# Layer 2's second product in seven products of sums, for two of its three superblocks

## The chip, the cores and the metric

The kernel runs on one core of a Trainium2 chip. Its engines work side by side, each through its own instructions in order: PE (TensorE) multiplies matrices, with its weight loads shown as a row of their own (PEld); DVE (VectorE), ACT (ScalarE) and POOL (GpSimd) work on elements; SP (SyncE) issues nearly all DMAs. The metric is the device time of one execution in microseconds (us). The kernel before takes 886.72 us, the median of 3 runs (886.31 to 887.06).

## The reference

Windowed attention over q, k, v (4 batches, 8 heads, 576 positions, 64 per head) gives x of 2304 tokens by 512. Two layers follow, each with weights 512x2048 and 2048x512:

```python
h = x @ w_in;  r = np.maximum(h, 0);  x = (r * r) @ w_out            # layer 1
h = x @ w_in2; g = h * np.tanh(log1p(exp(h)));  out = g @ w_out2     # layer 2
```

Everything is float32. A product of two float32 numbers is made of three matmuls: each operand is split into a high part (rounded to float32r) and a low part (the rest), and high x high, high x low and low x high are added.

## The kernel before, in words

The first 500 us are attention and layer 1, with the weights of layer 2 being unpacked and split beside them and stored to DRAM (`w1d`, `w2d`; `c_split`, `c_store`). Layer 2 is the loop at L1250. Its 2304 tokens are three superblocks of 768 (s = 0, 1, 2; "superblock one" is s = 0), and each superblock takes eight turns (g = 8s + m). Turn g makes one eighth of the hidden layer, two tiles of 128 features, for all 768 tokens.

- First product (`product`, L1121): it is already done as seven products of sums for eight, on 2x2 blocks: two tiles of features by two halves of 384 tokens (TH). Each product is 6 matmuls of 384 columns into one PSUM bank, and DVE and ACT combine the seven to four blocks. The sums of the weights come ready from `w1d` (`ring1_load`, four DMAs a turn: `ra`, `rb`, `rc`, `rd`, 1.84 MB together, for the turn after next); the sums of x are made ahead of a superblock by `x_prepare`, in 20 small jobs (`run_jobs`) of loads, POOL subtractions (L1055), ACT roundings (L1060) and DVE low parts (L1064).
- PSUM banks of the products: `p`, `h`, `o4`, `o5` in turn for g = 0, then `p` and `h` alone. The other six banks (`o0` to `o5`) hold the accumulators of the second product.
- Activation (`mish`, `mish_low`): ACT writes Mish twice, once rounded, once whole, and DVE subtracts (L1158) to get the low part.
- Second product (`o_chunk`, L1162): turn g does the 12 chunks of turn g-1, each 3 matmuls of 512 columns (L1172, L1173, L1174); stationary is a 128x128 piece of the activation, moving are the weights `vh`, `vl` (`ring2_load`). The list `share` spreads them between the seven products. So PE alternates between products of 6 matmuls and chunks of 3. Turn 24 has the last 12 chunks alone.
- Output: at the end of a superblock's last chunks (turn 8 and 16) `o_evac` copies six accumulators in pairs (ACT the even ones, DVE the odd ones) and stores them; `o_last` does it for the last superblock.

The order on every engine and on SP's queue is the order in which the program writes the instructions; waits are set by the data.

Of the kernel before, what the change touches and what calls it, by code (L numbers as in the profile page):

```python
# [8 lines left out]
F32 = mybir.dt.float32  # L9
# [9 lines left out]
P = 128  # L19
# [14 lines left out]
def two_layers(  # L34
# [37 lines left out]
    x1d = dp.tile([KC, P, NT], F32, name="x1d")  # L72
    w1d = dp.tile([FC // 2, P, 7 * 2 * 256], F32, name="w1d")
    w2d = dp.tile([FC, P, 2 * DM], F32, name="w2d")
    wsd = dp.tile([FC // 2, 2, P, 2 * DM], F32, name="wsd")

    def w_tile(dtype, hl, fc, name):
# [735 lines left out]
    def c_sums(i):  # L813
# [8 lines left out]
        tt(s3, a[:, 0:256], b[:, 0:256], op=ALU.subtract)  # L822
        tt(s4, a[:, 256:512], s2, op=ALU.subtract)

    def c_split(key, dst, first=0):
        f = wf.pop(key)[:, first:]
        n = f.shape[-1]
        hi = ap["c"].tile([P, DM], F32R, tag="c", name=f"c{len(wf)}", bufs=4)[:, 0:n]
        nc.scalar.copy(hi, f)
        late.append((f, hi, dst))  # L830

    def c_store():
        while kept:
            f, hi, dst = kept.pop(0)
            n = f.shape[-1]
            nc.sync.dma_start(out=dst[:, 0:n], in_=hi.bitcast(F32))
            nc.sync.dma_start(out=dst[:, n : 2 * n], in_=f)

# [5 lines left out]
    def c_tick1():  # L844

        i = made["at"]
        if i == 0:
            c_load(0)
        k, part = i // 4 * 4, i % 4
        if part == 3:  # L850
            c_split(k + 1, w2d[k // 2])
            a = wf[k]
            c_split(k, w1d[k // 4, :, 0:1024])
            wf[k] = a
        elif part == 0 and k:
            c_split(k - 2, w1d[k // 4 - 1, :, 1024:1536], 256)
            c_split((k - 2, 0), w1d[k // 4 - 1, :, 1536:2560])
        elif part == 1 and k:
            c_split(k - 1, w2d[k // 2 - 1])
            c_split((k - 2, 1), w1d[k // 4 - 1, :, 2560:3584])  # L860
        if i < NW:
            c_lower(i)
# [150 lines left out]

    def x_tile(s, name, part):
        k = 2 * KINDS.index(name) + part
        if s == 1:
# [91 lines left out]
    def ring2_load(m, g):  # L1108
        for e in range(2):
            k, pair_ = 2 * (g % 2) + e, []  # L1110
            for z, hl in enumerate("hl"):
                t = xp.tile([P, 512], F32R, tag=f"x{hl}{k}", name=f"v{hl}{g}_{e}")
                nc.sync.dma_start(
                    out=t.bitcast(F32), in_=w2d[2 * m + e, :, z * DM : (z + 1) * DM]
                )
                pair_.append(t)
            ring2[g, e] = pair_

# [1 line left out]

    def product(g, s, k, a, x):  # L1121
        banks = ((ps_b, "p"), (ps_h, "h"), (ps_b, "o4"), (ps_b, "o5"))
        pool, tag = banks[turns["p"] % (4 if g == 0 else 2)]
        turns["p"] += 1
        ps = pool.tile([P, 512], F32, tag=tag, name=f"p{k}_{g}")[:, 0:TH]
        w, (hi, lo) = ring1[g][a], xcs[s, x]
        terms = [(z, t, c) for z, t in ((0, hi), (0, lo), (1, hi)) for c in range(2)]
        for n, (z, t, c) in enumerate(terms):
            nc.tensor.matmul(  # L1129
                ps, w[:, z, c * P : (c + 1) * P], t[c], start=n == 0, stop=n == 5  # L1130
            )
        return ps
# [62 lines left out]
    def o_last(k):  # L1195

        ev = stg.tile([P, DM, 2], I32, tag="wraw", name=f"ev1_last{k}", bufs=4)
        ev = ev.rearrange("p c t -> p (c t)").bitcast(F32)
        b, at = 1 + (6 + k) // 4, (6 + k) % 4
        dst = out[b * S + at * P : b * S + (at + 1) * P, :]  # L1200
        if k != 2:
            (nc.scalar.copy if k % 2 else nc.vector.tensor_copy)(ev[:, 0:DM], acc[2, k])
            nc.sync.dma_start(out=dst, in_=ev[:, 0:DM])
            return
        h = stg.tile([P, DM], I32, tag="wf", name="ev1_half", bufs=4).bitcast(F32)[:, 0:256]
        nc.vector.tensor_copy(ev[:, 0:256], acc[2, k][:, 0:256])
        nc.sync.dma_start(out=dst[:, 0:256], in_=ev[:, 0:256])
        nc.scalar.copy(h, acc[2, k][:, 256:512])
        nc.scalar.dma_start(out=dst[:, 256:512], in_=h)

    j = NB - 1
    for fc in range(FC):
# [34 lines left out]


    todo = []
    for g in range(25):  # L1250
        s, m = divmod(g, 8)
        units_ = []
        if g == 0:
            relu2_b(pend)
            units_ = [lambda: m_out(*prev, 0), lambda: m_out(*prev, 1)]
            share = [0, 1, 1, 0, 0, 0, 0]
        else:
# [7 lines left out]
        if g == 24:  # L1265
            for h, (a, b) in ((1, (1, 2)), (0, (0, 3))):
                for c in range(3):
                    o_chunk(2, 23, todo[a], a, h, c)
                    o_chunk(2, 23, todo[b], 1 - a, h, c)
                    o_last(3 * h + c)  # L1270
            break
# [8 lines left out]
        def made_of(u, name):  # L1280
            a = mish(u, name)
            todo.append(a[0])
            lows.append(a)

        sub, add = ALU.subtract, ALU.add
        tt = nc.vector.tensor_tensor
        for k, (a, x) in enumerate(
            (
                ("a11", "b11"),
                ("a12", "b21"),  # L1290
                ("s2", "t2"),
                ("s3", "t3"),
                ("s1", "t1"),
                ("s4", "b22"),
                ("a22", "t4"),
            )
        ):
            ps = product(g, s, k, a, x)
            if k == 0:
                p1 = u_tile(f"p1_{g}")  # L1300
                nc.scalar.copy(p1, ps)
            elif k == 1:
                u = u_tile(f"c11_{g}")
                tt(u, ps, p1, op=add)
                made_of(u, f"g11_{g}")
            elif k == 2:
                u2 = u_tile(f"u2_{g}")
                tt(u2, ps, p1, op=add)
                done()
            elif k == 3:  # L1310
                u3 = u_tile(f"u3_{g}")
                tt(u3, ps, u2, op=add)
            elif k == 4:
                u = u_tile(f"c22_{g}")
                tt(u, ps, u3, op=add)  # L1315
                u4 = u_tile(f"u4_{g}")
                tt(u4, ps, u2, op=add)
                made_of(u, f"g22_{g}")
            elif k == 5:
                u = u_tile(f"c12_{g}")  # L1320
                tt(u, ps, u4, op=add)
                done()
                made_of(u, f"g12_{g}")
            else:
                u = u_tile(f"c21_{g}")
                tt(u, u3, ps, op=sub)
                done()
                made_of(u, f"g21_{g}")
            for _ in range(share[k]):
                units_.pop(0)()  # L1330
            if g == 0 and k == 3:
                m_evac(0, NB - 1)
            if m == 0 and g and k == 6:
                for n in range(3):
                    o_evac(s - 1, n)
            if 4 <= m < 8 and s < 2 and k in (1, 3, 4, 5, 6):
                run_jobs(1)
        done()
        if g == 0:
            jobs += x_prepare(1)  # L1340
        if g == 8:
            jobs += x_prepare(2)
        if g + 2 < 24:
            ring1_load((g + 2) % 8, g + 2)
        if g + 1 < 24:
            ring2_load((g + 1) % 8, g + 1)


# [83 lines left out]
```

## Time and profile before

| what | value |
|---|---|
| median of 3 runs | 886.72 us |
| profiled execution | 886.73 us, span 885.0 us, granted clock 0.999 |
| PE busy | 875.6 us, 99% of the span |
| DVE, ACT, POOL busy | 62%, 53%, 26% |
| DMA | 188 MB, mean 212 GB/s |

The span runs from the first to the last instruction; the execution's own time is 1.73 us longer. Busy times are sums over an engine's instructions. A PE that is busy all the time isn't a PE at its peak: the ends of matmuls are modelled, and what a matmul really takes is seen from the distance of one start to the next.

### The profile page before, as it was taken

Reading aid. Unit: us, or ns where it says so; the run is one execution under the profiler, and the core shown is the slowest. Engines: PE = TensorE matmul, PEld = TensorE weight load, DVE = VectorE, ACT = ScalarE, POOL = GpSimd, SP = SyncE. Lnnn points to the kernel's source line nnn. Section 1 sums busy time; section 2 is a strip of 40 time slices with the busy share of each in tenths; the row PEclk is TensorE's granted clock in tenths of the full one; section 3 lists DMA queues with packets and bytes.
Section 4 is the critical chain, followed back from the end, with each engine's and each line's share of the span. In section 5 each row is a group of like instructions: output and inputs, shape, how many; then the busy total and the mean of one; then the engine's idle time right before and its main releaser. Section 6 shows DMA issues by size and latency. Waiting matters only on the chain.

```text
span 885.0 us, 13898 instructions
## 1 busy us (share of the span) xinstructions
PE 875.6 (99%) x4642; PEld 753.7 (85%) x4642; DVE 549.6 (62%) x1221; ACT 471.7 (53%) x1108; POOL 226.0 (26%) x275
## 2 busy tenths in 40 slices
PE   8999999999999999999999999999999999999998
PEld 5588889998888788888888888888888888889987
DVE  6899997655697979977768243444444445433333
ACT  7888788775666666656655532333323334332332
POOL 4311144655665656642004000101000110000000
PEclk9999999999999999999999999999999999999999
DMA  8366694743875759754878765465494755566341
GB/s 301 96 220 202 201 317 149 261 153 124 280 241 176 241 171 326 273 171 157 302 235 287 292 243 211 171 236 188 144 319 145 270 181 204 188 230 223 142 156 71
DMA packets 90455, 188.03 MB, mean 212 GB/s; under 512 B 12304, under 2 KB 30352, under 8 KB 90384
## 3 DMA queue, kind: packets, MB, share of 16 engines
q1 hardware_dynamic: 90240, 187.02, 62.2%
q8 instruction: 37, 0.61, 0.3%
q14 instruction: 34, 0.28, 0.1%
q10 hardware_dynamic: 144, 0.13, 0.0%
HBM read 146.21 MB, written 40.89 MB: 211 GB/s over the span
## 4 chain that ended last, share of the span: by engine, by line
PE 84%; DVE 12%; issue 2%; ACT 1%; POOL 0%; DMA 0%; SPq 0%; DVEq 0%; POOLq 0%; ACTq 0%
PE p L1129 20%; PE h L561 17%; PE acc L1174 8%; PE acc L1173 8%; PE acc L1172 7%; PE o L593 6%; PE o L589 6%; PE o L590 6%; PE o L499 3%; DVE wf L108 3%; DVE wl L128 2%; PE pt L423 1%; PE sc L328 1%; PE sc L327 1%; DVE wf L105 1%
## 5 line engine op out<-in xcount | busy, mean ns | idle before, releaser
L1152 ACT ACTIVATE g<-c 128x384 fp32r<-128x384 f32 x96 | 50.5, 526 | 222.2 <-DVE c L1315 124.4
L589 PE MATMUL o<-g,wh 128*128 128x512 f32 (+1 forms) x320 | 118.5, 377 | 0.0
L590 PE MATMUL o<-g,wl 128*128 128x512 f32 (+1 forms) x320 | 115.9, 369 | 0.0
L1174 PE MATMUL acc<-vh,g 128*128 128x512 f32 x288 | 114.3, 397 | 0.0
L1173 PE MATMUL acc<-vl,g 128*128 128x512 f32 x288 | 113.8, 395 | 0.0
L1172 PE MATMUL acc<-vh,g 128*128 128x512 f32 x288 | 112.1, 389 | 0.0
L1055 POOL TENSOR_TENSOR t<-xb,xb 128x384 f32<-128x384 f32 x12 | 13.5, 1137 | 291.6 <-DMA xb<-x1d 230.1
L628 ACT ACTIVATE r<-h 128x512 f32<-128x512 f32 (+1 forms) x80 | 44.1, 552 | 81.3 <-PE h L561 77.6
L647 DVE TENSOR_TENSOR g<-gg,g 128x512 fp32r<-128x512 f32 (+1 forms) x80 | 64.0, 799 | 30.1 <-ACT g L642 21.2
L561 PE MATMUL h<-xh,wh 128*128 128x512 f32 (+1 forms) x320 | 81.5, 376 | 0.0
L593 PE MATMUL o<-g,wh 128*128 128x512 f32 (+1 forms) x320 | 79.5, 370 | 0.1
L561 PE MATMUL h<-xl,wh 128*128 128x512 f32 (+1 forms) x320 | 79.0, 369 | 0.0
L561 PE MATMUL h<-xh,wl 128*128 128x512 f32 (+1 forms) x320 | 78.8, 368 | 0.0
L459 POOL TENSOR_SCALAR_AFFINE_SELECT pT<-p 128x128 f32<-128x128 f32 (+2 forms) x80 | 53.8, 694 | 79.2 <-ACT p L447 78.9
L589 PEld LDWEIGHTS o<-g,wh 128*128 128x128 f32 x320 | 60.5, 189 | 9.8 <-issue 0.5
L590 PEld LDWEIGHTS o<-g,wl 128*128 128x128 f32 x320 | 60.4, 189 | 9.3
L593 PEld LDWEIGHTS o<-g,wh 128*128 128x128 f32 x320 | 56.5, 189 | 11.5 <-DVE g L647 1.5
L381 ACT ACTIVATE p<-p,st 128x128 f32<-128x128 f32 (+1 forms) x144 | 59.1, 413 | 13.2 <-DVE st L366 12.8
L561 PEld LDWEIGHTS h<-xl,wh 128*128 128x128 f32 x320 | 56.9, 189 | 10.5
L561 PEld LDWEIGHTS h<-xh,wl 128*128 128x128 f32 x320 | 56.9, 189 | 10.1
L257 POOL TENSOR_TENSOR ulo<-uraw,uhi 128x256 fp32r<-128x256 f32 (+1 forms) x48 | 47.0, 979 | 69.7 <-ACT uhi L256 47.1
L1174 PEld LDWEIGHTS acc<-vh,g 128*128 128x128 f32 x288 | 53.9, 187 | 11.5
(119 smaller groups left out, 1811.0 us busy)
## 6 DMA issues: line engine op xcount, KB each, us to landing
wraw<-in_w SPq DMA_DIRECT2D x64, 512.0 KB, 4.5
ra<-w1d SPq DMA_DIRECT2D x24, 512.0 KB, 5.9
rc<-w1d SPq DMA_DIRECT2D x24, 512.0 KB, 4.2
rd<-w1d SPq DMA_DIRECT2D x24, 512.0 KB, 5.9
vh<-w2d SPq DMA_DIRECT2D x48, 256.0 KB, 6.2
vl<-w2d SPq DMA_DIRECT2D x48, 256.0 KB, 6.3
uraw<-in_qkT SPq DMA_DIRECT2D x24, 320.0 KB, 4.7
uraw<-in_qkT SPq DMA_DIRECT2D x24, 256.0 KB, 5.4
```

The lines of the kernel that those rows point to most:

```text
L381: nc.scalar.activation(probs(i, s), probs(i, s), AF.Exp, bias=u.st[:, s : s + 1], scale=-1.0, accum_out=u.st[:, sums + s : sums + 1 + s],)
L459: nc.gpsimd.affine_select(out=u.pT[:, 0:heads, k : 2 * n : 2, :][:, :, a:], in_=p[:, 0:heads, a:n], pattern=[[0, heads * (n - a)], [0, P / ...
L561: nc.tensor.matmul(ph[:, 0:n], w[:, c * P : (c + 1) * P], xs[j, c][k][:, 0:n], start=t == 0, stop=t == len(terms) - 1,)
L589: nc.tensor.matmul(o, wh[:, ws], g[:, 0, r], start=start, stop=False)
L590: nc.tensor.matmul(o, wl[:, ws], g[:, 0, r], start=False, stop=False)
L593: nc.tensor.matmul(o, wh[:, ws], g[:, 1, r], start=False, stop=stop)
L647: nc.vector.tensor_tensor(g[:, 1, 0:n], gg[:, 0:n], g[:, 0, 0:n].bitcast(F32), op=ALU.subtract)
L1129: nc.tensor.matmul(ps, w[:, z, c * P : (c + 1) * P], t[c], start=n == 0, stop=n == 5)
L1152: nc.scalar.activation(t[:, 0, :], u, AF.Mish)
L1172: nc.tensor.matmul(o, hi, wh, start=first, stop=False)
L1173: nc.tensor.matmul(o, hi, wl, start=False, stop=False)
L1174: nc.tensor.matmul(o, lo, wh, start=False, stop=last)
```

## The change: what it does

Superblock one stays as it was. For superblocks two and three (s = 1, 2) the chunks of the second product are taken out of the turns; the second product gets a phase of its own (`products2`) behind the superblock's eight turns, and is made of seven products of 384 tokens by 1024 features by 256 outputs.

- The sums of the second weights (`t1` to `t4`) are made in turns 1 to 8 from the weights that superblock one has loaded (`t_prepare`: POOL sums, two ACT copies, two DVE subtractions, four stores a turn) and stored to `t2d`. `w2d` is laid out by halves of 256 columns, so its stores and superblock one's loads go in pieces of half the size.
- In superblocks two and three, Mish is written once, whole, into 16 block tiles. The sums of activations are made by POOL: `sums3` (two operations an eighth) in the turns, `sums_2` and `sums_4` in the phase. `high2` (ACT) and `low2` (DVE) split what the matmuls read.
- The phase has 56 steps q (7 products by 8 eighths). A step is 9 matmuls of 256 columns (3 token chunks by 3 terms), one load of weights 8 steps ahead (`t_load`, 256 KB), one `high2` 6 steps ahead, one `low2` 4 steps ahead, and in the first 16 steps one POOL sum. `combine` adds the seven products up from PSUM.
- The products of turns 9 to 23 take four banks in turn instead of two. x of the third superblock is prepared in the phase of the second one.

```diff
+    def t_prepare(m, k):                      # turn g = 1..8, m = g - 1, k = 0..6
+        ...
+                nc.gpsimd.tensor_tensor(b, h, l, op=ALU.add)           # k = 0, two of 512
+        ...
+                nc.gpsimd.tensor_tensor(o, a, b, op=sub)               # k = 1, 2, two of 256 each
+        elif k in (3, 4):
+            ...
+            nc.scalar.copy(hi, t_parts["t", z])
+        elif k == 5:
+            for z in range(2):
+                t, hi = t_parts["t", z], t_parts["h", z].bitcast(F32)
+                nc.vector.tensor_tensor(t, t, hi, op=sub)
+        else:
+            ...
+                    nc.sync.dma_start(out=dst.rearrange("k p c -> p k c"), in_=halves(src))
+    def sums3(s, m):
+        ...
+        nc.gpsimd.tensor_tensor(t, a, b, op=ALU.subtract)
+        nc.gpsimd.tensor_tensor(b, b, c, op=ALU.add)
+    def sums_2(s, m):
+        t = s3s[s, m]
+        nc.gpsimd.tensor_tensor(t, block(s, A21, m), block(s, A11, m), op=ALU.subtract)
+    def sums_4(s, m):
+        t = block(s, A21, m)
+        nc.gpsimd.tensor_tensor(t, block(s, A12, m), s3s[s, m], op=ALU.subtract)
+    ORDER2 = (("s3", "t3"), ("s1", "t1"), ("s2", "t2"), ("s4", "b22"), ("a11", "b11"), ("a12", "b21"), ("a22", "t4"))
+    def low2(s, q):                           # five tiles in turn
+        ...
+        nc.vector.tensor_tensor(lo, left(s, q), hi.bitcast(F32), op=ALU.subtract)
+    def terms2(s, q, o, c):
+        m = q % 8
+        hi, lo = (t[:, c * P : (c + 1) * P] for t in his[s, q])
+        w = ts2[s, q]
+        for z, (a, b) in enumerate(((hi, w[:, 0:256]), (hi, w[:, 256:512]), (lo, w[:, 0:256]))):
+            nc.tensor.matmul(o[c], a, b, ...)
+    def products2(s):
+        sums3(s, 7)
+        for q in range(3, 6):
+            high2(s, q)
+        low2(s, 3)
+        if s == 1:
+            jobs.extend(x_prepare(2))
+        owed = None
+        for n in range(7):
+            last = s == 2 and n == 6
+            o = bank2(s, n, last)
+            for m in range(8):
+                q = 8 * n + m
+                if last:
+                    continue
+                for c in range(3):
+                    terms2(s, q, o, c)
+                ...
+                    t_load(s, q + 8)
+                if q < 8:
+                    sums_2(s, q)
+                elif q < 16:
+                    sums_4(s, q - 8)
+                if q + 6 < 56:
+                    high2(s, q + 6)
+                if q + 4 < 56:
+                    low2(s, q + 4)
+                if m == 1 and owed:
+                    combine(*owed)
+                    owed = None
+                if m == 6:
+                    flush()
+                if s == 1 and q >= 4 and q % 2 == 0:
+                    run_jobs(1)
+            if last:
+                combine(*owed)
+                flush()
+                tail2(s, o)
+                return
+            owed = s, n, o
+        combine(*owed)
+    def tail2(s, o):                          # the last product, token chunk by token chunk
+        ...
+        for c in range(3):
+            for m in range(8):
+                terms2(s, 48 + m, o, c)
+            at = slice(c * 256, (c + 1) * 256)
+            nc.vector.tensor_tensor(t[:, at], t[:, at], o[c], op=ALU.subtract)
+            put(s, 1, 0, t, (c,))
@@ product
-        pool, tag = banks[turns["p"] % (4 if g == 0 else 2)]
+        pool, tag = banks[turns["p"] % (2 if 0 < g < 9 else 4)]
@@ the loop over turns
-    for g in range(25):
+    for g in range(24):
...
         def made_of(u, name):
+            if s:
+                a, e = blocks2[s, BLK[name[1:3]], m // 2], m % 2
+                nc.scalar.activation(a[:, e, :], u, AF.Mish)
+                return
...
-            if m == 0 and g and k == 6:
+            if g == 8 and k == 6:
                 for n in range(3):
-                    o_evac(s - 1, n)
+                    o_evac(0, n)
...
+            if 0 < g < 9:
+                t_prepare(g - 1, k)
...
+            if s and m and k == 0:
+                sums3(s, m - 1)
+            if s and m in (3, 4, 5, 6) and k in (1, 4):
+                t_load(s, 2 * (m - 3) + (k == 4))
+            if s and m == 7 and k in (2, 4, 6):
+                high2(s, k // 2 - 1)
+                low2(s, k // 2 - 1)
...
+        if s and m == 7:
+            products2(s)
```

## Rows read from the trace of the kernel before

**Rows 1.** Busy times by stretch: length, PE, PEld, DVE, ACT, POOL, clock, DMA share, GB/s.
```profile
560.00:600.00 40.00, 40.00 (x201) 35.90 (x200) 17.66 (x34) 13.74 (x28) 4.00 (x4) 1.00 0.69 243
```
**Rows 2.** The chain that ended last, 820 to 885 us, by line.
```profile
by line: PE p L1129 38.2%; PE acc L1174 19.0%; PE acc L1173 18.9%; PE acc L1172 18.6%; DVE ev_last L1206 0.7%; ACT ev_half L1208 0.6%; issue 0.1%
```
**Rows 3.** Timeline (start us, us, engine, line): turn 9's start, turn 24, the end.
```profile
637.59 1.21 PE L1129 MATMUL p<-x_b,ra 128*128 128x384 f32 x6
...
873.83 0.39 PE L1172 MATMUL acc<-vh,g 128*128 128x512 f32 x1
...
881.08 0.39 PE L1174 MATMUL acc<-vh,g 128*128 128x512 f32 x1
...
882.37 0.37 ACTq L1209 DMA_DIRECT2D out_x<-ev_half  x1
```
**Rows 4.** Timeline of PE in turn 0: products that follow one another.
```profile
508.39 1.20 PE L1129 MATMUL p<-x_t,rc 128*128 128x384 f32 x6
509.43 1.20 PE L1129 MATMUL p<-x_b,rd 128*128 128x384 f32 x6
```
**Rows 5.** Timeline of PE in layer 1: matmuls of 256 columns, first and eighth.
```profile
154.19 0.28 PE L589 MATMUL o<-g,wh 128*128 128x256 f32 x1
...
155.03 0.28 PE L590 MATMUL o<-g,wl 128*128 128x256 f32 x1
```
**Rows 6.** Timeline of weight loads, same stretch.
```profile
154.07 0.19 PEld L589 LDWEIGHTS o<-g,wh 128*128 128x128 f32 x1
154.19 0.19 PEld L590 LDWEIGHTS o<-g,wl 128*128 128x128 f32 x1
```
**Rows 7.** Timeline at the end of turn 8: copies and stores of superblock one, then ring1.
```profile
637.79 1.29 DVE L1182 COPY ev<-acc 128x512 f32<-128x512 f32 x2 [0.37 <-PE acc L1174]
...
638.57 0.96 SPq L1193 DMA_DIRECT2D out_x<-ev  x2
...
642.12 2.44 SPq L1188 DMA_DIRECT2D out_x<-ev  x4
...
644.65 0.54 SPq L1094 DMA_DIRECT2D ra<-w1d  x1
```
**Rows 8.** The page, part 6: KB each, median us from issue to landing.
```profile
ra<-w1d SPq DMA_DIRECT2D x24, 512.0 KB, 5.9
```
**Rows 9.** Timeline of POOL and DVE, layer 1: both with work queued.
```profile
463.56 2.44 POOL L1055 TENSOR_TENSOR t<-xb,xb 128x384 f32<-128x384 f32 x2 [52.88 <-PE o L593]
463.74 1.39 DVE L805 SCALAR_TENSOR_TENSOR wf<-wraw,wf 128x512 int32<-128x512 int32 x1
465.16 1.39 DVE L808 SCALAR_TENSOR_TENSOR wf<-wraw,wf 128x512 int32<-128x512 int32 x1
465.97 1.46 POOL L1055 TENSOR_TENSOR t<-xb,t 128x384 f32<-128x384 f32 x1
466.59 1.13 DVE L820 TENSOR_TENSOR s<-wf 128x256 f32<-128x256 f32 x1
467.50 1.09 POOL L1055 TENSOR_TENSOR t<-t,xb 128x384 f32<-128x384 f32 x1
467.75 1.13 DVE L821 TENSOR_TENSOR s<-s,wf 128x256 f32<-128x256 f32 x1
```
**Rows 10.** The same engines, 12 us later.
```profile
476.04 2.00 POOL L1055 TENSOR_TENSOR t<-xb,xb 128x384 f32<-128x384 f32 x1 [7.45 <-DVE x_t L1064]
476.48 0.69 DVE L866 TENSOR_TENSOR wf<-wf,c 128x512 f32<-128x512 f32 x1
```
**Rows 11.** Timeline of POOL and DVE in turn 4 of layer 2.
```profile
569.01 2.00 POOL L1055 TENSOR_TENSOR t<-xb,xb 128x384 f32<-128x384 f32 x2 [85.62 <-DMA xb<-x1d]
569.46 0.56 DVE L1315 TENSOR_TENSOR c<-p,u 128x384 f32<-128x384 f32 x1 [1.88 <-PE p L1129]
...
572.07 1.02 POOL L1055 TENSOR_TENSOR t<-t,xb 128x384 f32<-128x384 f32 x1
572.37 1.13 DVE L1158 TENSOR_TENSOR g<-c,g 128x384 fp32r<-128x384 f32 x1
```

More of the change, by code (lines that the diff above doesn't have):

```diff
@@ L1193, in o_evac @@
         nc.sync.dma_start(out=dst, in_=ev)
[L1195 to L1209, printed above, removed]
+    t_parts = {}
@@ new lines, in sums_2, with left @@
+    def sums_2(s, m):
[5 more added lines that the diff above has]
+    ORDER2 = (("s3", "t3"), ("s1", "t1"), ("s2", "t2"), ("s4", "b22"), ("a11", "b11"), ("a12", "b21"), ("a22", "t4"))
+    def left(s, q):
+        n, m = divmod(q, 8)
+        b = {"s1": A21, "s4": A21, "a11": A11, "a12": A12, "a22": A22}.get(ORDER2[n][0])
+        return s3s[s, m] if b is None else block(s, b, m)
@@ new lines, in high2 @@
+    def high2(s, q):
+        name = f"hi{s}_{q}"
+        if q < 3:
+            tag = ("st1", "st2", "st3")[q]
+            hi = ap["x"].tile([P, TH], F32, tag=tag, name=name).bitcast(F32R)
+        else:
+            hi = u_tile(name).bitcast(F32R)
+        nc.scalar.copy(hi, left(s, q))
+        his[s, q] = [hi]
+    def low2(s, q):
+        k, name = q % 5, f"lo{s}_{q}"
+        if s == 2 and q > 52:
+            lo = ap["x"].tile([P, TH], F32, tag=f"st{q - 52}", name=name).bitcast(F32R)
+        elif k < 3:
+            lo = ap["x"].tile([P, TH], F32R, tag="lo", name=name, bufs=3)
+        else:
+            lo = gp.tile([P, 512], F32, tag=("r", "gg")[k - 3], name=name)
+            lo = lo.bitcast(F32R)[:, 0:TH]
+        (hi,) = his[s, q]
+        nc.vector.tensor_tensor(lo, left(s, q), hi.bitcast(F32), op=ALU.subtract)
+        his[s, q].append(lo)
@@ new lines, in t_load @@
+    def t_load(s, q):
+        n, m = divmod(q, 8)
+        b = ORDER2[n][1]
+        if s == 2 and q > 53:
+            t = rp.tile([P, 1024], F32R, tag="ra", name=f"tt{s}_{q}")[:, 0:512]
+        else:
+            tag = f"x{'hl'[q % 2]}{q // 2 % 4}"
+            t = xp.tile([P, 512], F32R, tag=tag, name=f"tt{s}_{q}")
+        if b[0] == "t":
+            src = t2d[int(b[1]) - 1, m]
+        else:
+            src = w2d[2 * m + int(b[1]) - 1].rearrange("p (d c) -> p d c", d=2)[:, int(b[2]) - 1]
+        nc.sync.dma_start(out=t.bitcast(F32), in_=src)
+        ts2[s, q] = t
@@ new lines, in terms2, with bank2 @@
+    def terms2(s, q, o, c):
[3 more added lines that the diff above has]
+        for z, (a, b) in enumerate(((hi, w[:, 0:256]), (hi, w[:, 256:512]), (lo, w[:, 0:256]))):
+            nc.tensor.matmul(
+                o[c],
+                a,
+                b,
+                start=m == 0 and z == 0 and c in o[3],
+                stop=m == 7 and z == 2 and c in o[4],
+            )
+    def bank2(s, n, last):
+        if last:
+            b = [ps_o.tile([P, 512], F32, tag=f"o{c}", name=f"m{s}_{n}_{c}") for c in range(2)]
+            b.append(ps_b.tile([P, 512], F32, tag="o4", name=f"m{s}_{n}_2"))
+            return [t[:, 0:256] for t in b] + [(0, 1, 2), (0, 1, 2)]
+        k = n % 2 * 2
+        a, b = (ps_o.tile([P, 512], F32, tag=f"o{k + z}", name=f"m{s}_{n}_{z}") for z in range(2))
+        return [a[:, 0:256], a[:, 256:512], b[:, 0:256], (0, 2), (1, 2), a, b]
@@ new lines, in rows, with put, flush, combine @@
+    def rows(s, h, c):
+        q = 6 * s + 3 * h + c
+        b, at = 1 + (q - 6) // 4, (q - 6) % 4
+        return slice(b * S + at * P, b * S + (at + 1) * P)
+    def put(s, h, d, t, parts=range(3)):
+        for c in parts:
+            dst = out[rows(s, h, c), d * 256 : (d + 1) * 256]
+            nc.sync.dma_start(out=dst, in_=t[:, c * 256 : (c + 1) * 256])
+    puts = []
+    def flush():
+        while puts:
+            put(*puts.pop(0))
+    def combine(s, n, o):
+        tt, add, sub = nc.vector.tensor_tensor, ALU.add, ALU.subtract
+        two_ = ((o[5], slice(0, 512)), (o[6][:, 0:256], slice(512, 768)))
+        def fresh(k):
+            t = stg.tile([P, DM, 2], I32, tag="wraw", name=f"c2_{s}_{k}", bufs=4)
+            sums2[k] = t.rearrange("p c t -> p (c t)").bitcast(F32)[:, 0:768]
+            return sums2[k]
+        def each(f):
+            for ps, at in two_:
+                f(ps, at)
+        if n == 0:
+            t = fresh("a")
+            each(lambda ps, at: nc.scalar.copy(t[:, at], ps))
+        elif n == 1:
+            a, b, c = sums2["a"], fresh("b"), fresh("c")
+            each(lambda ps, at: nc.scalar.copy(b[:, at], ps))
+            each(lambda ps, at: tt(c[:, at], ps, a[:, at], op=add))
+        elif n == 2:
+            for k in "cba":
+                t = sums2[k]
+                each(lambda ps, at: tt(t[:, at], ps, t[:, at], op=add))
+        elif n == 3:
+            t = sums2["b"]
+            each(lambda ps, at: tt(t[:, at], ps, t[:, at], op=add))
+        elif n == 4:
+            d = fresh("d")
+            each(lambda ps, at: nc.scalar.copy(d[:, at], ps))
+            for k, h in (("c", 1), ("b", 0), ("a", None)):
+                t = sums2[k]
+                each(lambda ps, at: tt(t[:, at], ps, t[:, at], op=add))
+                if h is not None:
+                    puts.append((s, h, 1, t))
+        elif n == 5:
+            t = sums2["d"]
+            each(lambda ps, at: tt(t[:, at], ps, t[:, at], op=add))
+            puts.append((s, 0, 0, t))
+        else:
+            t = sums2["a"]
+            each(lambda ps, at: tt(t[:, at], t[:, at], ps, op=sub))
+            puts.append((s, 1, 0, t))
@@ new lines, in products2 @@
+    def products2(s):
[12 more added lines that the diff above has]
+                if last:
+                    continue
+                for c in range(3):
+                    terms2(s, q, o, c)
+                if s == 2 and q == 40:
+                    t_load(s, 54)
+                    t_load(s, 55)
+                if q + 8 < (56 if s == 1 else 54):
+                    t_load(s, q + 8)
[14 more added lines that the diff above has]
+                    run_jobs(1)
+            if last:
+                combine(*owed)
[4 more added lines that the diff above has]
+        combine(*owed)
@@ L1211, in two_layers @@
+    def tail2(s, o):
+        t = sums2["a"]
+        for q in range(54, 56):
+            high2(s, q)
+        for q in range(52, 56):
+            low2(s, q)
+        for c in range(3):
[4 more added lines that the diff above has]
+            put(s, 1, 0, t, (c,))
     j = NB - 1
@@ L1264, in two_layers @@
             share = [2, 2, 1, 2, 2, 1, 2]
[L1265 to L1271, printed above, removed]
+        else:
+            share = [0] * 7
         if g == 0:
@@ L1283, in made_of @@
             lows.append(a)
+        if s and m % 2 == 0:
+            for b in range(4):
+                blocks2[s, b, m // 2] = block_tile(s, b, m // 2)
         sub, add = ALU.subtract, ALU.add
```

71 lines of the change are left out of this document (60 added, 11 removed).

## The prediction

> **What bounds the kernel now.** I read the busy times of stretches of layer 2 first, then the chain, and last the timelines. In a 40 us stretch of layer 2 PE is busy all of it at a granted clock of 1.00 (2.4 GHz), with DVE at 44%, ACT at 34%, POOL at 10% and DMA at 0.69 [rows 1]. The chain agrees: but for 1.4%, its last 65 us are the products and the chunks [rows 2]. So a change gains what it takes from PE's stream of matmuls, as long as PE then waits for nothing; that is what has to be checked, since PE waits for almost nothing today.
>
> What a matmul costs is read from start to start. Products that follow one another take 1.04 us for 6 matmuls of 384 columns, 173 ns each [rows 4]. Matmuls of 256 columns take (155.03 - 154.19) / 7 = 120 ns [rows 5]. Matmuls of 512 columns take (881.08 - 873.83) / 32 = 226.6 ns in turn 24 [rows 3].
>
> **The gross gain.** From the first product of turn 9 at 637.59 to the end of the last matmul (881.08 + 0.23) the old PE stream takes 243.7 us [rows 3]. In its place come 15 turns of 7 products, 105 x 1.04 = 109.2, and two phases of 7 x 8 x 9 = 504 matmuls of 256 columns, 1008 x 0.120 = 121.0 [rows 4, 5]: 230.2 in all, 13.5 less. By the same prices the old stream would be 109.2 + 576 x 0.2266 = 239.7; the other 4.0 is what the alternation of products and chunks costs, and I count it as gone. Bounds of the new matmul's price: 120 ns, or what a matmul pays in today's turns on top: 4.0 over the 1170 matmuls of 15 turns, 3.4 ns, which makes 3.5 of 1008. I take 120: same size and type in rows 5, beside busy engines.
>
> Here a rule speaks against the change. The weight load is 188 ns long in its row, yet loads start 120 ns apart, so they lie beside the matmuls [rows 6]. The Trainium skill ("TensorE: Matmul & The Clock Gate", "LDWEIGHTS (loading the stationary operand)" and "Measured speedup vs the span model") gives 107 ns for a load of 128 columns and lets it overlap a matmul in flight only for another row group; by it I estimate 107 + 107 ns per matmul, 95 us over 1008 more than by the rows. Rows 5 and 6 contradict it.
>
> **What PE will wait for.**
>
> *Turn 9, 2.2 us.* Nine turns have made 63 products, and 63 mod 4 = 3, so turn 9's first product goes to bank `o5`, still accumulator 5 of superblock one. `o_evac` has DVE copy accumulators 1, 3 and 5 in that order, and accumulator 1 ends with the last matmul before 637.59. DVE starts at 637.79 and takes 1.29 for two [rows 7], 0.65 each: `o5` is free at 639.73 instead of 637.59. Before, the banks were `p` and `h` and this was hidden.
>
> *Turn 10, 1.8 us.* SP issues six output stores, then ring1 for turn 10 at 644.65 [rows 7]. Afterwards the last four stores start some 2.3 us earlier (a third copy waited for a buffer that Mish no longer takes), and behind them stand the four stores of `t_prepare`, 4 x 0.6 (2.44 / 4). `ra` goes out at about 644.6 as before, but turn 10 now begins at 639.8 + 7.28 = 647.1. At a median landing of 5.9 [rows 8] it comes at 650.5, 3.4 late; with an empty queue, at half of that time, 0.4. I take 1.8. From then on a turn needs 1.84 MB in 7.28 us, 252 GB/s, with `t_load` 288 over a superblock; 243 GB/s take 0.69 of the DMA engines, so some 350 are there [rows 1]. Hidden.
>
> *The port, 15.6 us.* This decides. With both engines loaded, POOL's subtraction of 384 columns and DVE's operations with two inputs in SBUF run one at a time. DVE's 463.74 takes 1.39, and each of the next three ends only after a POOL operation has ended; POOL's last three start before a DVE operation has ended and finish 0.9 after it [rows 9]. Four pairs take 463.56 to 468.88, 5.32, so 1.33 to 1.35 a pair, for DVE operations of 384 columns on the mean: POOL 0.92, DVE 0.43. In layer 2 it is the same: L1158, two SBUF inputs, takes 1.13 and ends 0.41 after POOL's at 573.09; L1315, with one input in PSUM, takes 0.56 beside POOL [rows 11]. The Trainium skill ("SBUF — State Buffer", "SBUF: two separate sides") states this as an exclusive lock of a shared port pair; what it leaves open is who goes next when both wait.
>
> `low2` has two SBUF inputs; so have POOL's sums. `combine` and the products' sums read PSUM and go free. A step of the phase lasts 9 x 0.120 = 1.08 and needs one `low2`; but from `sums3(7)` on POOL has 18 sums queued (2 + 8 + 8), none of which waits for PE. While they last, one `low2` comes every 1.35, and PE falls back 0.27 a step. The lead of `low2` is small at the start, since `low2` of step 2 stands behind the eighth turn's last Mish and POOL's first sum (0.3 late). Third superblock: 18 steps x 0.27 + 0.3 = 5.2. Second superblock: `x_prepare` adds four POOL sums, so 22 cycles, 30 us; and from step 10 on DVE has its low parts in between, two SBUF inputs too, three of which each take a whole cycle: 19 x 0.27 + 3 x 1.35 + 0.3 = 9.5; its second four sums come around step 30 and cost about 0.9 of the lead. 10.4. Below: if DVE, having an operation ready, always goes before POOL, as once in 476.48 [rows 10], POOL's sums move into the gaps. The third superblock then loses 0.4; in the second the last sum, which step 31 needs, comes after 22 x 0.92 and some 41 low parts x 0.43, 37.9 against 31 x 1.08 = 33.5, and I allow as much again for ACT, whose splits stand in order behind those of x: 8.0. Above: with POOL at its free duration of 1.02 [rows 11] a cycle is 1.45 and both grow by 0.10 / 0.27, to 14.3 and 7.1. I take alternation, which rows 9 show four times.
>
> *The end, -0.2 us.* `tail2` needs four `low2` and a `combine` in its first 3 us: 0.3 late. After the last matmul's start the old kernel needs 885.0 - 881.08 = 3.9, with two copies in a row before the last store is issued at 882.37 [rows 3]; now one subtraction of 256 columns: 0.5 less.
>
> *Costed at nothing.* Turns 1 to 8 get 6 POOL, 2 ACT and 2 DVE operations and 4 stores each. Their turn is 15.7 us long with DVE and ACT more than half idle [rows 1], and x's sums run there today without a wait of PE [rows 1, 11]. Without that cover, DVE's two would cost at most 8 x 1.3 = 10. A second Mish and one DVE subtraction per block go, from engines with slack: nothing gained. The split layout of `w2d` doubles the number of pieces and not the bytes: 0 with DMA at 0.69.
>
> **The sum.** -13.5 + 2.2 + 1.8 + 15.6 - 0.2 = +5.9. Against the profiled execution (span 885.0, and 1.73 around it, 886.73; the median is 886.72) that is 892.6 us.
>
> **Rivals.**
> - *DVE goes first.* The port costs 8.4: 885.4. For it rows 10; against it rows 9, where POOL gets its turn each time. Decides if `low2` rows of the first 20 steps last 0.5 and POOL's 1.5.
> - *The port costs nothing (faster).* POOL's sums drift behind the splits, or the lead of 4 to 5 low parts carries PE over: port 0.3, sum -9.4, 877.3. For it: DVE is needed for only 0.43 of each 1.08. Against it: POOL's 0.92 and DVE's 0.43 make 1.35 in every step, whoever is first, until the sums are done. It decides if fewer than some 6 steps run at more than 1.1.
> - *Slower still.* The new matmuls pay the 3.4 ns for their three-term pattern, or the turns of 7.28 us wait for ring1 by 0.23 each: 3.5 on the forecast, 896.1. For it: the 4.0 of today's turns, and 288 of some 350 GB/s. Against it: rows 5, and the share in rows 1.
> - *Weight loads in series.* If each matmul waits for its own load, 0.19 and not 0.12 is the pitch: 1008 x 0.07 = 71 on the forecast, 963. It is the mechanism of the skill's rule on loads. Rows 6 speak against it.
>
> **How the numbers follow.** Chances: forecast 0.46, DVE first 0.18, port free 0.24, slower still 0.10, weight loads 0.02. 0.2% of the time, 1.8 us, is about what a measurement can tell from no change: faster is under 884.9, slower over 888.5. Faster: 0.24 from the free port, 0.09 from DVE first, 0.04 from an overestimated forecast, 0.37. Same: 0.07 of DVE first and 0.04 of the forecast, 0.11. Slower: the rest, 0.52. Signs differ between the cases, so the forecast's own range is 888 to 897 (port 12 to 19, turn 10 0.4 to 3.4, not both at one end). The range for 8 in 10 is 876.5 to 898: it leaves out the lower part of the free port, the weight loads and the ends.
>
> **What would show it.** In the new trace: `terms2` matmuls 120 ns apart; PE idle 2.2 us before turn 9's first product, released by a DVE copy; `low2` at some 1.3 us a row in the first 20 steps of each phase and 0.56 later, PE released by it in each of these steps; the second superblock's phase 70 us long, the third's 65, against 60.5 without a wait. The prediction is wrong if the phases take 61 us, if `low2` does not lengthen beside POOL's sums, or if the products of turns 9 to 23 wait for ring1 or a bank in turn after turn.

## The result, and the profile after

The changed kernel takes 897.59 us (median of 4 runs, 893.8 to 898.25), the kernel before 886.89 (886.31 to 888.19): a ratio of 1.011, 95% interval 1.008 to 1.014. It is slower, by 10.7 us. The forecast was 892.6, slower as the likeliest sign, with 888 to 897 as its own range and 876.5 to 898 as the range for 8 in 10: the time lies in the wider one, 0.4 below its end, and 0.6 above the narrower. The profiled execution, the longest of the four, took 898.25 us with a span of 895.9, 10.9 more than the span before; the trace is accounted against these 10.9.

PE's waits, summed over the whole span (what waits, for whom: us in all, times, longest):

```profile
PE p L1139 <- DMA ra<-w1d: 3.9, 1, 3.9
PE m L1326 <- DVE lo L1303: 3.7, 3, 1.2
...
PE p L1139 <- DVE ev L1192: 2.0, 1, 2.0
...
PE p L1139 <- DVE c L1578: 1.4, 3, 0.7
```

All four are new; the first three stand in the prediction's sum, the fourth (behind the ends of turns 4 to 7) was costed at nothing. The list by waits is too short, though: a matmul that comes late because its weight load waited for `low2` is booked on PEld, and a slow clock is no wait at all. So I measure the losses in the timeline, from start to start.

The gross gain is there as forecast. First the timeline (start, us) of two products of turn 10, then the busy times of a stretch of the second superblock's phase (columns as in [rows 1]):

```profile
659.99 1.20 PE L1139 MATMUL p<-x_t,rd 128*128 128x384 f32 x6
661.03 1.20 PE L1139 MATMUL p<-x_t,rc 128*128 128x384 f32 x6
```

```profile
740.00:769.00 29.00, 29.00 (x244) 29.00 (x243) 22.89 (x44) 14.04 (x30) 7.08 (x4) 1.00 0.82 263
```

Products follow one another in 1.04 us as in [rows 4], and 244 of the new matmuls take 29 us, 119 ns each, as in [rows 5]; the numbers of loads (PEld) and matmuls (PE) are the same but for one. No turn of the third superblock waits for ring1 or for a bank: its eight turns, from 769.25 to 827.50, take 58.25, 7.28 each.

Now the end of turn 8, turn 9 and turn 10, the lines that answer to [rows 3] and [rows 7]. PE first, then SP's queue:

```profile
640.46 0.40 PE L1184 MATMUL acc<-vh,g 128*128 128x512 f32 x1
642.84 2.38 PE L1139 MATMUL p<-x_b,ra 128*128 128x384 f32 x12 [1.98 <-DVE ev L1192]
...
649.22 1.21 PE L1139 MATMUL p<-x_t,rb 128*128 128x384 f32 x6
654.37 4.18 PE L1139 MATMUL p<-x_b,ra 128*128 128x384 f32 x12 [3.95 <-DMA ra<-w1d]
658.35 1.80 PE L1139 MATMUL p<-x_t,rc 128*128 128x384 f32 x6
659.99 1.20 PE L1139 MATMUL p<-x_t,rd 128*128 128x384 f32 x6
```

```profile
642.73 3.32 SPq L1198 DMA_DIRECT2D out_x<-ev  x4
646.10 0.58 SPq L1240 DMA_DIRECT2D t2d<-th  x1
...
648.03 0.46 SPq L1240 DMA_DIRECT2D t2d<-t  x1
648.58 0.66 SPq L1106 DMA_DIRECT2D ra<-w1d  x1
```

Turn 9 starts 2.15 us after the last chunk's matmul ends (640.46 + 0.23 to 642.84). Turn 10 should have started at 649.22 + 1.04 = 650.26 and starts at 654.37, 4.11 late, 5.79 after its `ra` was issued. Behind this wait 18 matmuls take 5.62 us (654.37 to 659.99) in place of 3 x 1.04 = 3.12, another 2.50. That is the clock, as the busy times of this stretch, and of the first 12 matmuls alone, show:

```profile
650.00:660.00 10.00, 6.05 (x22) 5.76 (x21) 1.17 (x3) 2.05 (x4) 1.99 (x2) 0.66 1.02 366
654.40:658.30 3.90, 3.90 (x12) 3.90 (x13) 0.00 (x0) 0.48 (x1) 0.00 (x0) 0.50 1.02 403
```

The third number from the end is the mean granted clock, where 1.00 is 2.4 GHz and 0.50 the lower level of 1.2 GHz: 0.66 over the 10 us, and 0.50 over the first 12 matmuls behind the wait. The number behind it is the busy share of the DMA engines, here as good as all of them.

In the phases the reader should look at DVE and POOL together, at the start of the second superblock's phase:

```profile
702.70 7.04 DVE L1303 TENSOR_TENSOR lo<-s,hi 128x384 fp32r<-128x384 f32 x6 [0.99 <-ACT hi L1290]
709.67 9.09 DVE L1303 TENSOR_TENSOR lo<-a,hi 128x384 fp32r<-128x384 f32 x7
718.68 1.37 DVE L1076 TENSOR_TENSOR x_b<-xb,x_b 128x384 fp32r<-128x384 f32 x1
```

```profile
704.14 9.04 POOL L1270 TENSOR_TENSOR s<-a,a 128x384 f32<-128x384 f32 x7
713.15 2.61 POOL L1067 TENSOR_TENSOR t<-xb,xb 128x384 f32<-128x384 f32 x2
```

Seven `low2` take 718.68 - 709.67 = 9.01 us, 1.29 each, and seven POOL sums 713.15 - 704.14 = 9.01, also 1.29 each: one of each in turn, as in [rows 9]. PE needs a `low2` every 1.08. The phase of the second superblock takes 68.70 us (700.55 to 769.25), that of the third 65.14 (827.50 to 892.52 and one matmul); 504 x 0.120 = 60.48 would be without loss, so 8.2 and 4.7 are lost.

The whole account of the span, in us: -13.5 gross; +2.4 in turns 1 to 8 (from layer 2's first product to the last chunk's matmul 501.40 to 637.36 before, 502.06 to 640.46 now: 135.96 and 138.40); +2.15 turn 9; +4.1 and +2.5 turn 10 and its clock; +8.2 and +4.7 in the phases; -0.5 at the end (3.4 from the last matmul's start in place of 3.9); +0.7 ahead of layer 2, which stays unexplained (its first product starts between 500.4 and 502.6 in all traces of this study); +0.1 in turn 9's first products. The sum is +10.9.

### The profile page after: what moved, and what is told of

Same layout as the page of the kernel before. It is cut to its first block, busy times and chain, and to the rows that moved or that the text cites. A ratio compares the mean times of both kernels' runs of the same rounds, so it can differ in the third digit from the quotient of the medians.

```text
span 895.9 us, 15580 instructions
## 1 busy us (share of the span) xinstructions
PE 875.0 (98%) x5074; PEld 770.3 (86%) x5074; DVE 649.5 (73%) x1320; ACT 500.8 (56%) x1177; POOL 359.4 (40%) x387
## 4 chain that ended last, share of the span: by engine, by line
PE 78%; DVE 12%; DMA 4%; issue 2%; ACT 2%; SPq 1%; POOL 0%; DVEq 0%; POOLq 0%; ACTq 0%
PE h L562 17%; PE p L1139 16%; PE m L1326 13%; PE o L594 6%; PE o L590 6%; PE o L591 6%; PE o L500 3%; PE acc L1184 2%; PE acc L1183 2%; PE acc L1182 2%; DMA vl<-w2d 1%; PE pt L424 1%; DVE wf L109 1%; PE sc L329 1%; PE sc L328 1%
## 5 line engine op out<-in xcount | busy, mean ns | idle before, releaser
L1326 PE MATMUL m<-tt,hi 128*128 128x256 f32 x672 | 122.7, 283 | 0.2
L1326 PEld LDWEIGHTS m<-tt,hi 128*128 128x128 f32 x672 | 104.4, 191 | 0.7 <-issue 0.5
L1326 PE MATMUL m<-tt,lo 128*128 128x256 f32 x336 | 98.9, 294 | 4.0 <-DVE lo L1303 3.7
L1528 ACT ACTIVATE a<-c 128x384 f32<-128x384 f32 x64 | 33.5, 526 | 80.3 <-DVE c L1567 42.7
L1326 PEld LDWEIGHTS m<-tt,lo 128*128 128x128 f32 x336 | 64.0, 191 | 10.1 <-DVE lo L1303 9.7
L590 PEld LDWEIGHTS o<-g,wh 128*128 128x128 f32 x320 | 60.5, 189 | 9.8 <-issue 0.5
L1265 POOL TENSOR_TENSOR s<-a,a 128x384 f32<-128x384 f32 x16 | 16.6, 1037 | 124.4 <-ACT a L1528 124.4
```

The source lines that it names most:

```text
L590: nc.tensor.matmul(o, wh[:, ws], g[:, 0, r], start=start, stop=False)
L1326: nc.tensor.matmul(o[c], a, b, start=m == 0 and z == 0 and c in o[3], stop=m == 7 and z == 2 and c in o[4],)
L1528: nc.scalar.activation(a[:, e, :], u, AF.Mish)
```

## The experiments

Each ratio is to the kernel before, with its 95% interval.

**No sums.** The calls of `sums_2` and `sums_4` left out.

```diff
-                if q < 8:
-                    sums_2(s, q)
-                elif q < 16:
-                    sums_4(s, q - 8)
```

> The changed kernel without POOL's 16 sums in each phase (`sums_2` and `sums_4` are left out, so products three and four multiply unsummed blocks). Theory (POOL's sums and DVE's `low2` exclude each other): both phases lose their waits; the second superblock's phase falls from 68.7 to about 62 (x's four POOL sums stay), the third's from 65.0 to about 61, and the time falls by some 10 us, to about 887. Rival (the splits come late for another reason: ACT's order, the five low tiles, DVE's own load): the phases stay at 68 and 65, since neither the splits nor their number change.

Measured 885.11 us, 0.9976 (0.9962 to 0.9989). The phases take 61.2 and 61.4 us. So the 16 sums of each phase cost 7.5 and 3.8 us, 11.3 of the 12.9 that the phases lost. The other 0.7 and 0.9 are there without them, with x's sums still in the second superblock's phase.

**The same sums for nobody.** POOL does as many subtractions of the same size, into a tile that nothing reads (`sums_4` is changed in the same way).

```diff
-        t = s3s[s, m]
-        nc.gpsimd.tensor_tensor(t, block(s, A21, m), block(s, A11, m), op=ALU.subtract)
+        t = spare(s)
+        nc.gpsimd.tensor_tensor(t, block(s, A12, m), block(s, A11, m), op=ALU.subtract)
```

> As the run without the sums, but POOL does 16 subtractions of the same size per phase from two block tiles into a tile that nothing reads (the products read unsummed blocks, as in that run). Theory of the exclusion: the phases are as long as with the real sums, 68 and 64 to 65, and `low2` takes 1.3 us a row beside them. Rival (PE waits because the sums' data come late): phases of 61 to 62, as nothing waits for these sums.

Measured 895.42 us, 1.0096 (1.0081 to 1.0111); phases of 69.2 and 64.9 us. The loss is back though nothing depends on the sums: it is that POOL works there, not that its results come late.

**Turn 9's bank.** One more product is counted ahead of turn 9, so that its first product goes to bank `p` (64 mod 4 = 0) and not to `o5`.

```diff
+        if g == 9:
+            turns["p"] += 1
```

> One product number is skipped at turn 9, so that its first product goes to bank `p` instead of `o5`. Theory: the 2.0 us wait of PE before turn 9's first product goes. Turn 10 begins 2.1 us earlier and waits for `ra` as much longer (6 instead of 3.95), with the clock as low behind it: same time as the changed kernel within 1 us. Rival (the two waits add up independently): 2 us faster.

Measured 896.80 us, 1.011 (1.0094 to 1.0127): 0.8 below the changed kernel's median, less than its four runs differ among themselves. Turn 9 starts right behind the chunks, and turn 10 waits the longer:

```profile
646.27 1.21 PE L1139 MATMUL p<-x_t,rb 128*128 128x384 f32 x6
654.21 4.03 PE L1139 MATMUL p<-x_b,ra 128*128 128x384 f32 x12 [6.74 <-DMA ra<-w1d]
```

Turn 10 starts at 654.21 against 654.37: the two waits stand one behind the other, and the transfer sets the end of both.

**Ring1 for turn 10 ahead of the stores.**

```diff
             if g == 8 and k == 6:
+                ring1_load(2, 10)
                 for n in range(3):
                     o_evac(0, n)
...
-        if g + 2 < 24:
+        if g + 2 < 24 and g != 8:
```

> Ring1 of turn 10 is issued before superblock one's output stores and before the four stores of weight sums, instead of behind them. Theory: `ra` lands before turn 10, the 3.95 us wait and the 2.5 us at half clock behind it go: 6.4 us faster, about 891. Rival (DMA bandwidth, not the order, makes `ra` late): the wait moves to another part of ring1 or to turn 11, less than 2 us gained.

Measured 890.48 us, 1.0047 (1.003 to 1.0064): 7.1 us gained. No wait for `ra` is left; the one for the bank stays, and in this trace the clock falls behind it:

```profile
644.75 3.47 PE L1139 MATMUL p<-x_b,ra 128*128 128x384 f32 x12 [1.98 <-DVE ev L1192]
648.02 1.71 PE L1139 MATMUL p<-x_t,rc 128*128 128x384 f32 x6
649.56 1.20 PE L1139 MATMUL p<-x_t,rd 128*128 128x384 f32 x6
```

18 matmuls in 4.81 us in place of 3.12. This profiled execution took 894.41 us, the longest of six and 3.9 above their median, so the loss of clock need not be in the others. In the changed kernel's own trace the same wait of 1.98 cost next to nothing of clock (642.84 to 645.06 is 2.22 for 12, in place of 2.08).

**Both.**

> Both edits around turn 9 at once: the products of turn 9 begin in banks o4 and o5, and turn 10's ring1 load goes out ahead of the three stores. The one with the early load gained 7.1 us and still held the 1.98 us wait for the bank, with about 1.7 us of half clock behind it. If that rest comes from the bank wait, this gives 890.5 - 3.7 = 886 to 888 us with full clock from turn 9 on. Rival: as with the bank edit alone, another wait takes the place of the bank's, and the time stays at 890 to 891.

Measured 888.27 us, 1.0016 (1.0007 to 1.0026). Turn 9 begins with bank `p`, as in the run on the bank alone. A wait of 0.9 for turn 11's `ra` is all that is left around there, and the clock stays at 1.00. With turn 10's transfer out of the way the bank edit is worth 2.2 us, about the wait itself, where alone it brought nothing that stands clear of the scatter. Turns 9 and 10 together cost 9.3 us.

**The sums on DVE.**

```diff
-        nc.gpsimd.tensor_tensor(t, block(s, A21, m), block(s, A11, m), op=ALU.subtract)
+        nc.vector.tensor_tensor(t, block(s, A21, m), block(s, A11, m), op=ALU.subtract)
...
-        nc.gpsimd.tensor_tensor(t, block(s, A12, m), s3s[s, m], op=ALU.subtract)
+        nc.vector.tensor_tensor(t, block(s, A12, m), s3s[s, m], op=ALU.subtract)
```

> The 16 subtractions per phase of sums_2 and sums_4 run on DVE in place of POOL, at the same steps. Theory (POOL and DVE shut each other out): nothing is left to shut out, and what remains is DVE's own load: 0.55 + 0.55 us in a step of 1.08, and in the second superblock six low parts of x by 0.55 us in the same steps, of which four steps' lead covers some. So the phases fall from 68.7 and 65.1 to 60.5 to 64 and 60.5 to 61.5 us, and the time to 886 to 889. Rival: low2 is late because of the number of elementwise operations, wherever they run; then the time stays at 895 to 899.

Measured 887.02 us, 0.9998 (0.9988 to 1.0007): 10.6 gained by giving the late engine more to do. Two of its lines in the third superblock's phase:

```profile
828.69 0.55 DVE L1303 TENSOR_TENSOR lo<-a,hi 128x384 fp32r<-128x384 f32 x1
829.16 0.55 DVE L1270 TENSOR_TENSOR s<-a,a 128x384 f32<-128x384 f32 x1
829.62 0.55 DVE L1303 TENSOR_TENSOR lo<-a,hi 128x384 fp32r<-128x384 f32 x1
```

`low2` alone is 829.16 - 828.69 = 0.47 us from start to start, and a sum and a `low2` together take 829.62 - 828.69 = 0.93 on DVE, where `low2` beside POOL's sum takes 1.29. The phases take 62.6 and 61.3 us.

**All three, spread.** Both edits at turn 9, and the sums on DVE in two of three steps over 24 steps, x's jobs from step 14.

```diff
-                if q < 8:
-                    sums_2(s, q)
-                elif q < 16:
-                    sums_4(s, q - 8)
+                if q < 12 and q % 3 != 2:
+                    sums_2(s, q - q // 3)
+                elif 12 <= q < 24 and q % 3 != 2:
+                    sums_4(s, q - 12 - (q - 12) // 3)
...
-                if s == 1 and q >= 4 and q % 2 == 0:
+                if s == 1 and q >= 14 and q % 2 == 0:
```

> Both edits around turn 9, and the sums on DVE spread over 24 steps (two in three) with x's jobs from step 14 on. If the terms add: 887 - 12.7 (the two phases' loss) + 0 to 1.5 = 874 to 876 us, phases of 60.5 to 62 us, and no wait of a multiplication for low2 over 0.5 us. Rival: DVE takes POOL's place as the late engine, with 0.92 us of work of 1.08 in each step and x's low parts beside it: phases of 63 to 66 us, 880 to 886.

Measured 878.87 us, 0.9909 (0.9894 to 0.9924), 3 to 5 above what I expected of it: the second superblock's phase still takes 62.6 us (the third's 61.3), and the sums on DVE had brought 10.6 and not 12.7.

**And turns 1 to 8.** The two DVE subtractions of `t_prepare` apart, behind steps 4 and 6.

```diff
-        elif k == 5:
-            for z in range(2):
-                t, hi = t_parts["t", z], t_parts["h", z].bitcast(F32)
-                nc.vector.tensor_tensor(t, t, hi, op=sub)
-        else:
+        if k in (4, 6):
+            z = k // 2 - 2
+            t, hi = t_parts["t", z], t_parts["h", z].bitcast(F32)
+            nc.vector.tensor_tensor(t, t, hi, op=sub)
+        if k == 6:
```

> The one before, and in turns 1 to 8 the two DVE subtractions of t_prepare no longer stand together behind step 5, ahead of the subtraction that frees the next product's bank, but behind steps 4 and 6. If these two stood in the way, the 2.4 us that turns 1 to 8 lost come back: 872 to 874 us, and the last of the chunks' multiplications starts 2.0 to 2.6 us earlier. Rival: the loss comes from POOL's eight operations per turn, which hold DVE wherever its subtractions stand: same time as the one before, within 0.5 us.

Measured 876.92 us, 0.9885 (0.987 to 0.9899), 2.0 below the one before, and 3 to 5 above what I expected, as the one before was. From layer 2's first product to the last chunk's matmul it is 135.95 us (501.15 to 637.10), as in the kernel before the change, against 138.52 (501.46 to 639.98) in the run before. That is 2.6 less; the second superblock's phase, where nothing was changed, took 63.6 us in place of 62.6, and why is not known. In the changed kernel the place looks like this (DVE, then PE, at the end of turn 4):

```profile
574.61 2.94 DVE L1235 TENSOR_TENSOR t<-t,th 128x512 f32<-128x512 f32 x2
577.47 0.54 DVE L1578 TENSOR_TENSOR c<-u,p 128x384 f32<-128x384 f32 x1
```

```profile
578.07 1.00 PEld L1139 LDWEIGHTS p<-x_b,ra 128*128 128x128 f32 x6 [0.41 <-DVE c L1578]
```

Two operations of 1.43, lengthened beside POOL's sums of x, stand ahead of the subtraction that frees the bank of the next product but one. With one moved ahead and one behind it, `c` is made at 573.91 in place of 577.47 (layer 2 starts 0.9 earlier in this trace):

```profile
573.43 0.56 DVE L1076 TENSOR_TENSOR x_b<-xb,x_b 128x384 fp32r<-128x384 f32 x1 [0.76 <-ACT x_b L1072]
573.91 0.55 DVE L1580 TENSOR_TENSOR c<-u,p 128x384 f32<-128x384 f32 x1
```

**x's work late and off POOL.** In the second superblock's phase x's jobs run from step 24 on, five in eight steps, and x's own sums on DVE.

```diff
-                if s == 1 and q >= 14 and q % 2 == 0:
+                if s == 1 and q >= 24 and q % 8 in (0, 2, 3, 5, 6):
...
-                nc.gpsimd.tensor_tensor(t, b[x, c], b[y, c], op=ALU.subtract)
+                eng = nc.vector if s == 2 else nc.gpsimd
+                eng.tensor_tensor(t, b[x, c], b[y, c], op=ALU.subtract)
```

> The kernel with all corrections so far, and in the second superblock's phase x's jobs only from step 24 on, five in eight steps, with x's own four sums per half on DVE too: POOL then does nothing in the phase. The trace of the kernel with all corrections has two stretches there in which PE falls behind (0.88 us in 720 to 725, 1.00 us in 740 to 745, behind x's four POOL sums each), and a phase of 63.6 us against 61.4 for the third superblock. If the alternation with these eight sums is what is left, the phase falls to 61 to 62 us and the time to 874.5 to 876. Rival: DVE's load in the late steps (0.47 for low2 and some 0.6 for x in a step of 1.08, with combine beside it) brings the same wait again: 876.5 to 877.5.

Measured 878.44 us, 0.9914 (0.9898 to 0.9929): a miss. It is no faster than the one before (1.5 slower by the medians, with intervals that just touch), and the phase takes 64.3 us. Waits from 735 to 750 us in this run:

```profile
ACT x_b L1073 <- DMA xb<-x1d: 3.1, 2, 2.1
DVE t L1068 <- DMA xb<-x1d: 2.3, 2, 1.3
...
PE m L1327 <- DVE lo L1304: 1.4, 2, 1.2
```

With the jobs close together x's transfer is not there when its first operations come up, and on ACT and DVE these stand ahead of `high2` and `low2`. On POOL the wait for x's transfer, 18.7 us long in the run before, had no work of another kind behind it. What x's sums on DVE cost with their loads earlier was not tried.

The run before also shows something that the expectation passed over. In the two stretches in which PE falls behind there, POOL does nothing; its four sums of x are over by 715.4 and 738.9. DVE is busy all the time, and what stands ahead of the late `low2` is `combine` (the first of the two places; DVE, then PE):

```profile
719.45 1.01 DVE L1382 TENSOR_TENSOR c_c<-m,c_c 128x512 f32<-128x512 f32 x2
720.38 1.01 DVE L1382 TENSOR_TENSOR c_b<-m,c_b 128x512 f32<-128x512 f32 x2
721.31 1.01 DVE L1382 TENSOR_TENSOR c_a<-m,c_a 128x512 f32<-128x512 f32 x2
722.24 0.55 DVE L1303 TENSOR_TENSOR lo<-a,hi 128x384 fp32r<-128x384 f32 x1
```

```profile
722.83 0.38 PE L1326 MATMUL m<-tt,lo 128*128 128x256 f32 x1 [0.88 <-DVE lo L1303]
```

Six operations of `combine` hold DVE for 722.24 - 719.45 = 2.79 us, 2.6 steps, not long after POOL's sums of x had lengthened DVE's operations from 0.55 to 1.37. At the second place it is the same (737.97 to 740.76, and a wait of 0.99). Which of the two has to go, or both, no run tells: `combine` was never spread.

**Copies in place of sums.** As the second run, but POOL copies (one input) where it subtracted (two).

> As the run with POOL operations of the same size into a tile that nobody reads, but each is a copy with one input in place of a subtraction with two (sums_2 and sums_4 are left out, so the combinations of the last four products are not computed). If POOL and DVE shut each other out whatever POOL does, low2 still lengthens by the copy's own duration (no row for it; 0.5 to 1.0 us), the phases take 64 to 69 and 62.5 to 65 us, and the time is 888 to 895. Rival: only operations with two inputs in SBUF on both sides shut each other out; then low2 stays at 0.55 us, the phases at 61 to 62 as without any sums, and the time at 884 to 886.

Measured 884.55 us, 0.9978 (0.9967 to 0.9989), phases of 61.2 and 61.4 us. The time is the rival's, the rows are the theory's (DVE and POOL in the third superblock's phase):

```profile
826.25 5.51 DVE L1311 TENSOR_TENSOR lo<-a,hi 128x384 fp32r<-128x384 f32 x7
```

```profile
822.74 6.28 POOL L1278 COPY spare<-a 128x384 f32<-128x384 f32 x8
829.08 6.02 POOL L1282 COPY spare<-a 128x384 f32<-128x384 f32 x8
```

One `low2` and one copy still go in turn, 0.79 us a pair (5.51 / 7, 6.28 / 8), against 0.47 for a `low2` in a row of its own. But 0.79 is under the step's 1.08, so PE sees none of it. My expectation went wrong in the arithmetic: it added the copy's length to `low2`, and did not compare the pair with the step.

## Why the prediction was right, and where its terms were wrong

The sign and the main cause were right; the sum was 5.0 too low against the trace (+5.9 forecast, +10.9 measured). That the time still lies in the range for 8 in 10 is in part luck: the port's term was 2.7 too large and stood against 7.2 too little for turn 10 and turns 1 to 8. By its steps:

- *Gross gain, -13.5.* Right: 1.04 us a product and 0.119 to 0.120 a matmul held over 105 products and 1008 matmuls wherever PE did not wait. The rival with weight loads in series is out: 1008 loads, 191 ns long in the mean in their rows, lie beside matmuls 120 ns apart. The rule that a load overlaps a matmul in flight only for another row group stands in the Trainium skill ("TensorE: Matmul & The Clock Gate") under "The mechanism", whose text also lets a load for the background weight buffer go ahead; the estimate of 107 + 107 ns per matmul took the rule alone. The trace does not agree with it: 244 matmuls in 29 us are 119 ns each.
- *Port, 15.6.* Right in mechanism, too large by 2.7. A pair takes 1.29 and not 1.35, and the prediction's own sum with that comes near what was measured: 19 x 0.21 + 3 x 1.29 + 0.3 + 0.9 = 9.1 in the second superblock (8.2), 18 x 0.21 + 0.3 = 4.1 in the third (4.7). POOL's 16 sums of each phase account for 11.3 of the 12.9. The two runs with and without POOL's sums show that POOL's work alone is the cause, and the alternation held for some 20 pairs in a row, so DVE does not go first. (That rival's own sum was short: 37.9 - 33.5 = 4.4, and as much again makes 8.8, not 8.0, so it stood at 886.2 us.)
- *Turn 9, 2.2.* Right (2.15). What the prediction did not see is that it was no term of its own: turn 10's transfer would have ended both.
- *Turn 10, 1.8.* This is the step that failed most. It put `ra`'s issue 2.5 us ahead of turn 10; it was 1.7 ahead (648.58 to 650.26). Superblock one's last four stores began earlier behind the last chunk, as forecast (642.73 - 640.69 = 2.0 us in place of 642.12 - 637.59 = 4.5), but took 3.32 us to issue in place of 2.44 [rows 7]. I then took the middle between an empty queue and the median landing of [rows 8]; with a DMA share of 0.97 from 645 to 650 us and 1.01 from 650 to 654 the engines were not idle, and `ra` landed in 5.79, near the median, which made the wait 4.1. And I had no price for what a wait of this length does to the clock, 2.5 us more. 6.6 in all in place of 1.8; with turn 9's 2.15 that is 8.8, and the runs gave 9.3 back.
- *Turns 1 to 8, 0.* Wrong, 2.4. "DVE more than half idle" [rows 1] is a mean; the two subtractions stood together at the one place of the turn where PE waits for the next DVE result, and in turns 4 to 7 beside POOL's sums: x's in turns 4 and 6, which made them 1.43 us each, and those of the weights in turns 5 and 7, 1.15 each.
- *End, -0.2.* -0.5: the 0.5 less is there, the delay of 0.3 is not.

The Trainium skill ("SBUF — State Buffer", "SBUF: two separate sides") has the port as an exclusive lock that an instruction holds for its whole length. The traces agree that the two take turns, and differ on the length: 1.02 for POOL's subtraction by itself [rows 11] and 0.47 for `low2` would be 1.49 a pair, and it is 1.29; a copy of 0.71 (the median of its rows) and a `low2` would be 1.18, and it is 0.79.

What stays open: six traces have the wait of 1.98 us at turn 9 (the changed kernel, the runs without sums, with sums for nobody, with copies, with the sums on DVE, and with ring1 earlier). In the runs without sums and with ring1 earlier it was followed by about 1.7 us lost to the clock, in the other four by 0.1; nothing I ran tells the two apart. One of the changed kernel's four runs took 893.8 us and the others 897.5 to 898.3; why is not known. And of the second superblock's phase some 2 to 3 us (62.6 to 63.6 against 60.5) are left; where PE falls behind there, `combine` stands ahead of `low2` behind x's sums, and which of them is the cause is not shown.

The version with all corrections takes 876.92 us and beats both kernels: 10.0 below the kernel before, 20.7 below the changed one.

## What to carry to other kernels

When PE runs at its limit, price a new operation of POOL by what it does to the DVE operation beside it, and compare the pair with the step in which PE needs one: 1.29 against 1.08 cost 11.3 us here, while 0.79 cost nothing, and doing both on DVE in 0.93 was cheaper than sharing. Where the end of the last wait does not depend on the first, waits that follow one another on the same engine are one wait: removing the first gains next to nothing until the last is gone, and a long one may take the clock along. An engine's mean idle share says nothing about the one place in a turn where somebody waits for it; look there.

## What the hardware showed unexpectedly

- POOL subtractions of 384 columns and DVE's two-input ones go strictly in turn, 1.29 us a pair for 1.01 and 0.47 alone; with POOL copies, 0.71 long in their rows, it is 0.79. In both cases a pair is shorter than its two parts, so a part of each instruction's length lies beside the other.
- A wait of PE of 3.95 us was followed by 18 matmuls in 5.62 us in place of 3.12, the first 12 at a granted clock of 0.50; after one of 6.74 us 12 matmuls took 3.87 (654.21 to 658.08) in place of 2.08, and the next ones were at full speed. So the longer wait cost less clock, 1.8 us against 2.5.
